# Attention stage of a gated-mix kernel: which queue issues which transfer, gate rows of all blocks in one step, the last tile turned in one row

## Chip, cores, metric

The kernel runs on one core of one Trainium2 chip. The metric is the device time of one execution in microseconds (us). Engines are named as in the profile: PE is TensorE's matrix multiplication, PEld its weight load, DVE VectorE, ACT ScalarE, POOL GpSimd, SP SyncE, whose only work here is to issue DMAs.

## What is computed

`x` is 2048 tokens x 576. Branch A is a linear attention with 32 heads of 18 features, branch B a gated feed-forward layer of 4608 hidden features; a sigmoid of one logit per token mixes the two. Everything is float32.

```python
qkv = x @ wqkv                                  # per head: q, k, v
pq, pk = q @ w_phi, k @ w_phi                   # 18 x 18 per head
phi_q = concat([softmax(pq), softmax(-pq)])     # 36 features per head
phi_k = concat([softmax(pk), softmax(-pk)])
kv  = einsum("bhsf,bhsd->bhfd", phi_k, v);  z = phi_k.sum(over tokens)
num = einsum("bhqf,bhfd->bhqd", phi_q, kv)
den = einsum("bhqf,bhf->bhq", phi_q, z) + 1e-6
a = (num / den) @ wo
gate = x @ W_gate; h = gate * (gate > 0) * (x @ W_up); b = h @ W_down
g = sigmoid((x * gate_w).sum(-1))
out = g * a + (1 - g) * b
```

## The kernel before

**Stages.** The first part, to about 404 us, is the attention; the rest is the feed-forward layer, in which TensorE works almost without a pause (1222 of the last 1232 us). Tokens come in 16 tiles of 128 and in 4 blocks of 512; the blocks' attention is finished in the order 3, 0, 1, 2, so "block 0" below is the first in that order.

**Keys, values, query features.** Per tile TensorE projects keys, values and queries, VectorE and ScalarE make the softmax features, and `kv_step` sums the products of key features and values. The query features `e` of a tile (128 tokens x 1152) are needed with features on the partitions: `turn` transposes them in eleven pieces of 128 x 108 in three groups (4, 4 and 3) into PSUM, and ScalarE copies each group out. For the last four tiles that copy goes straight into the operand `ph` of the sums. For the first twelve it goes to a tile `et`, which a DMA stores to DRAM (`eT`, 594 KB each); `fetch` reads four of them back as one block's `ph` (four DMAs of 594 KB).

**Sums and division.** `sums` multiplies `ph` with the summed key-value products `kvm`: six results per block, in the order 4, 5, 3, 2, 1, 0. ScalarE copies each to SBUF (`R`, for the fifth `og`). The numerators stand in the rows of `R`, the denominators in a few rows between them; small DMAs of 4 to 12 KB collect the denominators into `dn` (SP's queue), and others, of 28 to 40 KB, bring rows that lie in `og` into the free rows of `R` (`R<-og`, GpSimd's queue). `gate_rows` spreads the block's gates over 128 x 128 (`gx`, VectorE) and TensorE transposes them. `invert` takes the reciprocal of `dn` on VectorE, multiplies it by the gate rows, changes its layout from 128 x 128 to 32 x 512 with one DMA of 64 KB (`kt<-dn`, SP's queue), and splits the result into a high and a low half, `rd` (ScalarE, then VectorE). `divide` spreads `rd` over the rows of `R` by a matmul with `spread`; VectorE multiplies, ScalarE and VectorE split the quotients into `oh` and `ol`. `first_out` and `project_out` multiply them with `wo`; `rows_out` copies the result to a tile `o` and stores it to DRAM as `att`, which the feed-forward part reads back much later. The tiles `o` (and `sb`, a row spread that is stored as `sbd`) come from the pool `tb_`, which has four buffers.

**Loads for the feed-forward part in the same stage.** `load_operand` reads sums of `x` back (`xr<-xt`, 768 KB each), `load_in_place` and `load_rests` read `xo<-xt` (512 KB) and `xr<-xt` (256 KB), `load_w` weights (`wr<-wgu`, 768 KB). All are issued by SP.

**What sets the order.** From the last tiles on the program is written out by hand inside `in_order`: TensorE, SP and GpSimd carry out their instructions exactly as written, and a DMA that has to wait for its data holds up all that stands behind it in its engine's queue. VectorE and ScalarE are ordered by a scheduler, apart from the places marked `after`. The piece of the written order around block 0's inversion reads:

```python
        turn(FIRST - 2, 2, turned(kv_bank(0)))
        g0 = gate_rows(0, kv_bank(1))
        fetch(BLOCKS[2], nc.gpsimd)
        final = query_steps(FIRST - 1, eng=nc.vector)
        next(final)
        invert(0, g0)
        ...
        sums(1, (4,), (kv_bank(0),))
        sums(1, (5,), (kv_bank(1),))
```

and the one that follows the last tile: `load_operand(0, 0)`, `load_operand(0, 1)`, `fetch(BLOCKS[3])`, `first_out(2)`, `sums(2, (4, 5))`, `divide(0, 0)`, `invert(1)`. Names in the profile are those of the tiles; a line is the one that issues the instruction (L382 the store of `et`, L421 the fetch, L542 and L544 `dn`, L546 and L549 `R<-og`, L571 `kt<-dn`, L573 `rd`, L737 `att`, L751 to L786 the loads of `x` sums, L804 `wr`).

Of the kernel before, what the change touches and what calls it, by code (L numbers as in the profile page):

```python
# [14 lines left out]
DH = D // H  # L15
# [68 lines left out]
def gated_mix_kernel(  # L84
# [102 lines left out]
    def softmax_parts(ps, out):  # L187

        p = ps[:, :, :D // 2].rearrange("p c (h f) -> p c h f", f=DH)
        mx = soft.tile([P, H], F32, name="mx")  # L190
        mn = soft.tile([P, H], F32, name="mn")
        by2 = lambda a: a.rearrange("p (c h) -> p c h", c=2)
        wide = lambda a: by2(a)[:, :, :, None].to_broadcast([P, 2, H // 2, DH])
        nc.vector.tensor_reduce(out=by2(mx), in_=p, axis=AX, op=ALU.max)
        nc.vector.tensor_reduce(out=by2(mn), in_=p, axis=AX, op=ALU.min)
        yield
        e = ep.tile([P, H, 2, DH], F32, name="e")
        e2 = e.rearrange("p (c h) s f -> p c h s f", c=2)
        tt(out=e2[:, :, :, 0], in0=p, in1=wide(mx), op=SUB)
        tt(out=e2[:, :, :, 1], in0=wide(mn), in1=p, op=SUB)  # L200
        nc.scalar.activation(e, e, AF.Exp)
        yield
        sm = soft.tile([P, H, 2], F32, name="sm")
        nc.vector.tensor_reduce(out=sm.rearrange("p h s -> p (h s)"), in_=e.rearrange("p h s f -> p (h s) f"),  # L204
                                axis=AX, op=ADD)
        out.extend((e, sm))
# [157 lines left out]
    def turn(t, b, ps=None):  # L364

        gg = QN[b]
        if ps is None:
            ps = pv1.tile([QK, 4, P], F32, name="ptr", tag="pv1")
        for i, g in enumerate(gg):
            nc.tensor.transpose(ps[:, i], flat(EQ[t])[:, QC[g]:QC[g] + QK], ident)  # L370
        if t >= FIRST:
            nc.scalar.activation(PH[t // 4][:, t % 4, gg.start:gg.stop], ps[:, :len(gg)], AF.Copy)
        else:
            if t not in ET:
                ET[t] = etp.tile([QK, NQ, P], F32, name="et")
            a = ET[t][:, gg.start:gg.stop], ps[:, :len(gg)]
            nc.scalar.activation(*a, AF.Copy)
        TURNED[t] = TURNED.get(t, 0) + 1
        if TURNED[t] == 3:
            EQ.pop(t)  # L380
            if t < FIRST:
                nc.sync.dma_start(eT[t * QK:(t + 1) * QK], ET.pop(t).rearrange("p g t -> p (g t)"))  # L382

# [67 lines left out]
    for t in range(2, NT - 2):  # L451
# [10 lines left out]
        if t == 12:  # L462
# [5 lines left out]
            kt_p = RS.enter_context(tc.tile_pool(name="kt_p", bufs=1, **R_))  # L468
            kt_ = kt_p.tile([P, NJ * QK + 120], F32, name="kt")
            kt = kt_[:, :NJ * QK].rearrange("p (g c) -> p g c", g=NJ)  # L470
# [56 lines left out]
    def sums(b, ii, pp_):  # L527
# [9 lines left out]
        for i, ps in zip(ii, pp_):  # L537
            n = P if i < NJ - 1 else QM
            og = (OG4[b] if i == 4 else R[:, i if i < 4 else 4])[:n]
            nc.scalar.activation(og, ps[:n], AF.Copy)  # L540
            if i < NJ - 1:
                nc.sync.dma_start(dn[4 * HG * i:4 * HG * (i + 1)], og[64 - QH:64 + QH])  # L542
            else:
                nc.sync.dma_start(dn[4 * HG * i:], og[:2])  # L544
            if i < 4:
                nc.gpsimd.dma_start(R[QG:QG + 2 * GAP, i], OG4[b][i // 2 * 74 + i % 2 * 20:][:20])  # L546
            elif i == 5:
                for r, c in ((0, 40), (14, 114)):
                    nc.gpsimd.dma_start(R[r:r + 14, 4], OG4[b][c:c + 14])  # L549
            if i == 0:  # L550
                PH.pop(BLOCKS[b])

    RD, OW = {}, {}

    def gate_rows(b, ps):

        c = 4 * BLOCKS[b]
        gx = rb.tile([P, H, 4], F32, name="gx", bufs=1)
        nc.vector.tensor_copy(gx, gs[:, None, c:c + 4].to_broadcast([P, H, 4]))
        nc.tensor.transpose(ps[:, :P], gx.rearrange("p h c -> p (h c)"), ident)  # L560
        return ps[:, :P]

    def invert(b, g=None):

        dn = DN.pop(b)
        if g is None:
            g = gate_rows(b, kv_bank(0))
        nc.vector.reciprocal(dn, dn)
        tt(out=dn, in0=g, in1=dn, op=MULT)
        d2 = kt_[:H, :TB]  # L570
        nc.sync.dma_start(d2, dn)  # L571
        rd = RD[b] = rb.tile([2 * H, TB], F32R, name="rd", bufs=1)
        nc.scalar.activation(rd[:H], d2, AF.Copy)  # L573
# [59 lines left out]
    with in_order(tc, nc, nc.tensor, nc.sync, nc.gpsimd):  # L633
# [48 lines left out]
        turn(FIRST - 2, 2, turned(kv_bank(0)))  # L682
        g0 = gate_rows(0, kv_bank(1))
        fetch(BLOCKS[2], nc.gpsimd)
        final = query_steps(FIRST - 1, eng=nc.vector)
        next(final)
        invert(0, g0)
        halves = last_of(nc, nc.scalar), last_of(nc, nc.vector)
        two = pp.tile([P, 2, TB], F32, name="po", tag="pp")
        sums(1, (4,), (kv_bank(0),))  # L690
        sums(1, (5,), (kv_bank(1),))
        sums(1, (3, 2), (two[:, 0], two[:, 1]))
        next(final)
# [3 lines left out]
        sums(1, (1,), (kv_bank(2),))  # L697
        sums(1, (0,), (pv1.tile([P, TB], F32, name="po", tag="pv1"),))
        divide(0, 3)
        two = pp.tile([P, 2, TB], F32, name="pw", tag="pp")  # L700
# [6 lines left out]
        two = pp.tile([P, 2, TB], F32, name="po", tag="pp")  # L707
        turn(FIRST - 1, 2, turned(kv_bank(0)))
        for b in range(2):
            turn(FIRST - 1, b, turned(two[:, b]))  # L710
        divide(0, 1)
# [9 lines left out]
    def root_rows(tb):  # L721

        sb = tb_.tile([P, TB], F32, name="sb", tag="tb")
        on_all_rows(kv_bank(0), sb, tb)
        nc.sync.dma_start(sbd[:, tb], sb)

    def rows_out(b, m, ps):
# [9 lines left out]
        (nc.sync if b == NTB - 1 else nc.gpsimd).dma_start(att[m * P:m * P + n, BLOCKS[b] * TB:(BLOCKS[b] + 1) * TB], o)  # L737

# [8 lines left out]

    def load_operand(hf, i):
        if i < len(SEQ):
            XR[hf, i] = xr.tile([P, 3, TB], F32, name="xr", tag="xr")  # L750
            nc.sync.dma_start(XR[hf, i], xt[:, hf, SEQ[i] - 1])  # L751

# [125 lines left out]
    def operand_ahead(i):  # L878
# [4 lines left out]
        if i == 0:  # L883
            load_operand(0, 2)

# [6 lines left out]
    with in_order(tc, nc, nc.tensor, nc.sync, nc.gpsimd):  # L892
        x0, x1, x2 = (operand_ahead(i) for i in range(3))
        load_operand(0, 0)
        load_operand(0, 1)
        fetch(BLOCKS[3])
        first_out(2, range(5))
        halves = two[:, 0], two[:, 1]
        sums(2, (4, 5), halves)
        divide(0, 0)  # L900
        invert(1)
        first_out(1, range(5))
        sums(2, (3, 2), halves)
        divide(1, 4)
        for m in range(5):
# [4 lines left out]
            if m == 3:  # L910
                divide(1, 2)
        sums(2, (1, 0), halves)
        divide(1, 1)
        divide(1, 0)
        for m in range(5):
            project_out(1, m)
            if m < 3:
                two = pp.tile([P, 2, TB], F32, name="po", tag="pp")
                sums(3, ORDER[2 * m:2 * m + 2], (two[:, 0], two[:, 1]))
            if m == 0:  # L920
                invert(2)
            else:
                divide(2, 5 - m)
# [4 lines left out]
            if m == 4:  # L928
                divide(2, 0)
                invert(3)  # L930
                whole(x1)
        for m in range(5):
# [630 lines left out]
```

## Time and profile before

| | |
|---|---|
| time, median of 3 runs | 1643.85 us (1640.85 to 1646.56) |
| the profiled execution | time 1644.79 us, span 1643.0 us, mean granted clock 0.984 |
| busy, of the span | PE 1594.9 us (97%), PEld 1325.0 (81%), DVE 1198.9 (73%), ACT 561.8 (34%), POOL 177.4 (11%) |
| DMA | 284.43 MB, mean 173 GB/s |
| chain that ended last | PE 87%, DVE 6%, DMA 3%, ACT 2% |

The profile is of one execution. An engine's busy time counts its compute instructions; DMA issues, waits and branches don't count. "Granted clock" is the share of full speed that TensorE had. The chain is followed back from the last instruction, at each step to what released it. A row with x4 stands for four instructions in a row of the same line, operation and shape.

### The profile page before, as it was taken

To read this page: it belongs to the slowest core of one execution; us is meant where nothing else is said; L and a number is where in the kernel's file an instruction comes from. 1 tells how busy PE (TensorE), PEld (TensorE's weight loads), DVE (VectorE), ACT (ScalarE), POOL (GpSimd) and SP (SyncE) were. 2 spreads that over 40 slices of the span, in tenths; PEclk is the share of its full clock that TensorE was granted. 3 is DMA by queue.
4 is the path that set the end of the run, shared out by engine and by line. 5 is a ranking of instruction groups with operands and counts; after the bars stand their busy time and mean duration, and the time that the engine had idled before them with its cause. 6 is when DMAs were issued, how large, how long until landed. Compare 5 with 4: busy or idle time off the path is not lost.

```text
span 1643.0 us, 20184 instructions
## 1 busy us (share of the span) xinstructions
PE 1594.9 (97%) x7823; PEld 1325.0 (81%) x7823; DVE 1198.9 (73%) x1856; ACT 561.8 (34%) x921; POOL 177.4 (11%) x261
## 2 busy tenths in 40 slices
PE   9998998788999999999999999999999999999998
PEld 8898995456888888888888887778888888888887
DVE  4898775346778787788777777667777677777777
ACT  4343334344333333333233234223232323223231
POOL 0128212110000000000000002111111111111110
PEclk9899998899999999999999999999999999999999
DMA  8154305428775566555654543554343434344342
GB/s 266 65 180 157 113 24 150 149 87 313 260 257 198 208 234 241 203 211 208 222 204 177 201 158 116 176 216 155 140 168 139 185 127 182 127 171 153 146 163 72
DMA packets 64587, 284.43 MB, mean 173 GB/s; under 512 B 7018, under 2 KB 17514, under 8 KB 55788
## 3 DMA queue, kind: packets, MB, share of 16 engines
q1 hardware_dynamic: 61532, 275.25, 45.9%
q0 software_dynamic: 2384, 6.86, 1.4%
q8 instruction: 61, 1.00, 0.2%
q10 hardware_dynamic: 576, 1.05, 0.2%
q14 instruction: 34, 0.28, 0.0%
HBM read 172.51 MB, written 109.21 MB: 171 GB/s over the span
## 4 chain that ended last, share of the span: by engine, by line
PE 87%; DVE 6%; DMA 3%; ACT 2%; issue 2%; POOL 0%; SPq 0%; DVEq 0%; ACTq 0%; POOLq 0%
PE cx L1060 27%; PE ca L1060 13%; PE pd L1100 12%; PE pd L1123 10%; PE cy L1060 7%; PE kv L175 3%; PE pq L175 2%; PE pm L1100 2%; PE pm L1123 2%; PE pk L175 2%; PE pw L175 1%; DMA kt<-dn 1%; PE pv L237 1%; DVE sm L204 1%; DMA wdr<-wd 1%
## 5 line engine op out<-in xcount | busy, mean ns | idle before, releaser
L1167 ACT ACTIVATE hh<-g 128x512 fp32r<-128x512 f32 x195 | 119.9, 624 | 459.2 <-DVE g L1217 289.9
L1138 DVE TENSOR_TENSOR ac<-pd,ac 128x512 f32<-128x512 f32 x238 | 164.0, 689 | 145.4 <-PE pd L1123 145.2
L1060 PE MATMUL cx<-xo,wb 128*128 128x512 f32 x1008 | 252.1, 393 | 4.3 <-DVE u L1342 3.5
L1060 PE MATMUL cx<-xo,ws 128*128 128x512 f32 x1008 | 252.5, 390 | 2.9 <-ACT g L1221 2.8
L1060 PE MATMUL ca<-xo,ws 128*128 128x512 f32 x1008 | 252.0, 389 | 0.6 <-DMA ws<-wsd 0.6
L1060 PEld LDWEIGHTS cx<-xo,wb 128*128 128x128 f32 x1008 | 190.1, 190 | 46.5 <-DVE u L1342 4.4
L1060 PEld LDWEIGHTS cx<-xo,ws 128*128 128x128 f32 x1008 | 189.0, 188 | 43.6 <-ACT g L1221 4.6
L1060 PEld LDWEIGHTS ca<-xo,ws 128*128 128x128 f32 x1008 | 189.4, 188 | 40.2 <-issue 1.0
L1100 PE MATMUL pd<-hh,wd 128*128 128x512 f32 x576 | 200.8, 389 | 0.0
L1123 PE MATMUL pd<-hh,wd 128*128 128x512 f32 x476 | 185.4, 390 | 0.0
L1106 DVE TENSOR_TENSOR ac<-pd,ac 128x512 f32<-128x512 f32 x144 | 99.0, 688 | 105.5 <-PE pd L1100 103.2
L1172 DVE TENSOR_TENSOR hl<-g,hh 128x512 fp32r<-128x512 f32 x195 | 136.2, 699 | 1.9 <-ACT hh L1167 0.2
L1221 ACT ACTIVATE g<-cx 128x512 f32<-128x512 f32 x144 | 84.6, 588 | 128.0 <-PE cx L1060 127.9
L1100 PEld LDWEIGHTS pd<-hh,wd 128*128 128x128 f32 x576 | 108.2, 188 | 22.5 <-DVE ac L1106 0.2
L1060 PE MATMUL cy<-xo,wb 128*128 128x512 f32 x504 | 125.9, 389 | 0.0
L1023 ACT ACTIVATE wd<-wdr 128x384 fp32r<-128x384 f32 (+1 forms) x106 | 62.3, 607 | 152.1 <-DMA wdr<-wd 152.1
L1100 PE MATMUL pd<-hl,wd 128*128 128x512 f32 x288 | 112.2, 390 | 1.0 <-ACT xo L792 1.0
L1060 PEld LDWEIGHTS cy<-xo,wb 128*128 128x128 f32 x504 | 94.7, 188 | 19.6
L1123 PEld LDWEIGHTS pd<-hh,wd 128*128 128x128 f32 x476 | 89.4, 188 | 18.6
L1123 PE MATMUL pd<-hl,wd 128*128 128x512 f32 x238 | 92.6, 389 | 0.0
L776 POOL TENSOR_TENSOR xo<-xr,xo 32x512 fp32r<-32x512 f32 x5 | 8.2, 1655 | 639.3 <-DVE xo L776 631.7
L1026 DVE TENSOR_TENSOR wd<-wdr,wd 128x384 fp32r<-128x384 f32 (+1 forms) x106 | 69.5, 670 | 5.4 <-ACT wd L1023 5.4
(247 smaller groups left out, 2606.1 us busy)
## 6 DMA issues: line engine op xcount, KB each, us to landing
wsd<-ws SPq DMA_DIRECT2D x34, 1280.0 KB
ws<-wsd SPq DMA_DIRECT2D x34, 1280.0 KB
wbd<-wb SPq DMA_DIRECT2D x34, 960.0 KB
wb<-wbd SPq DMA_DIRECT2D x34, 960.0 KB
wr<-wgu SPq DMA_DIRECT2D x36, 768.0 KB
wdr<-wd SPq DMA_DIRECT2D x36, 576.0 KB
eT<-et SPq DMA_DIRECT2D x12, 594.0 KB
xt<-xb SPq DMA_DIRECT2D x7, 768.0 KB
```

The lines of the kernel that those rows point to most:

```text
L175: nc.tensor.matmul(ps, w, m, start=i == 0, stop=i == len(pairs) - 1)
L204: nc.vector.tensor_reduce(out=sm.rearrange("p h s -> p (h s)"), in_=e.rearrange("p h s f -> p (h s) f"), axis=AX, op=ADD)
L1023: nc.scalar.activation(o[:, 0], a, AF.Copy)
L1026: tt(out=o[:, 1], in0=a, in1=o[:, 0].bitcast(F32), op=SUB)
L1060: nc.tensor.matmul(ps, w, v, start=first and m == 0, stop=m == len(pairs) - 1, skip_group_check=True)
L1100: nc.tensor.matmul(ps, w, v, start=k == 0 and (i < 2 or first), stop=k == len(mms) - 1 and (i < 2 or last), skip_group_check=True)
L1106: tt(out=a, in0=ps, in1=a, op=ADD)
L1123: mm = lambda ps, w, v, a, z: nc.tensor.matmul(ps, w, v, start=a, stop=z, skip_group_check=True)
L1138: tt(out=a, in0=ps, in1=a, op=ADD)
L1167: nc.scalar.activation(h, src, AF.Copy)
L1172: tt(out=l, in0=src, in1=h.bitcast(F32), op=SUB)
L1221: nc.scalar.activation(a, ps, AF.Copy)
```

## The change

Four things, all in the attention stage:

1. The gathers `R<-og` move from GpSimd's queue to SP's, in batches written out by a new function `gather`; the stores of `att` of all blocks are now SP's (before, only the last block's). The stores of `et` of tiles 10 and 11, the last fetch, the first three `xr<-xt` and the stores `sbd` move from SP's queue to GpSimd's.
2. The gate rows of all four blocks are made once, before block 0's inversion: GpSimd copies the gates into 128 x 512 (`gx`), TensorE makes four transposes, ScalarE copies the result into `gT`, the upper half of the tile whose lower half takes `kt<-dn`.
3. `invert` is cut in two, `invert` (to the DMA) and `split_inverse` (from `rd` on); for block 0, the two first sums of block 1 are written between them. For the other blocks the second follows the first directly.
4. For tile 11 the eleven transposes stand in a row and the three copies after them; before, each group's transposes were followed by its copy.

```diff
 
-        gg = QN[b]
-        if ps is None:
-            ps = pv1.tile([QK, 4, P], F32, name="ptr", tag="pv1")
-        for i, g in enumerate(gg):
-            nc.tensor.transpose(ps[:, i], flat(EQ[t])[:, QC[g]:QC[g] + QK], ident)
-        if t >= FIRST:
-            nc.scalar.activation(PH[t // 4][:, t % 4, gg.start:gg.stop], ps[:, :len(gg)], AF.Copy)
-        else:
-            if t not in ET:
-                ET[t] = etp.tile([QK, NQ, P], F32, name="et")
-            a = ET[t][:, gg.start:gg.stop], ps[:, :len(gg)]
-            nc.scalar.activation(*a, AF.Copy)
+        turn_all(t, [(b, pv1.tile([QK, 4, P], F32, name="ptr", tag="pv1") if ps is None else ps)])
+
+    def turn_all(t, bb):
+
+        for b, ps in bb:
+            for i, g in enumerate(QN[b]):
+                nc.tensor.transpose(ps[:, i], flat(EQ[t])[:, QC[g]:QC[g] + QK], ident)
+        for b, ps in bb:
+            gg = QN[b]
+            if t >= FIRST:
+                o = PH[t // 4][:, t % 4]
+            else:
+                if t not in ET:
+                    ET[t] = etp.tile([QK, NQ, P], F32, name="et")
+                o = ET[t]
+            nc.scalar.activation(o[:, gg.start:gg.stop], ps[:, :len(gg)], AF.Copy)
+        TURNED[t] = TURNED.get(t, 0) + len(bb) - 1
         TURNED[t] = TURNED.get(t, 0) + 1
         if TURNED[t] == 3:
             EQ.pop(t)
             if t < FIRST:
-                nc.sync.dma_start(eT[t * QK:(t + 1) * QK], ET.pop(t).rearrange("p g t -> p (g t)"))
+                (nc.sync if t < FIRST - 2 else nc.gpsimd).dma_start(eT[t * QK:(t + 1) * QK], ET.pop(t).rearrange("p g t -> p (g t)"))
 
...
             kt_p = RS.enter_context(tc.tile_pool(name="kt_p", bufs=1, **R_))
-            kt_ = kt_p.tile([P, NJ * QK + 120], F32, name="kt")
+            kt_ = kt_p.tile([P, 2 * TB], F32, name="kt")
+            gT = kt_[:, TB:]
             kt = kt_[:, :NJ * QK].rearrange("p (g c) -> p g c", g=NJ)
...
                 nc.sync.dma_start(dn[4 * HG * i:], og[:2])
-            if i < 4:
-                nc.gpsimd.dma_start(R[QG:QG + 2 * GAP, i], OG4[b][i // 2 * 74 + i % 2 * 20:][:20])
-            elif i == 5:
-                for r, c in ((0, 40), (14, 114)):
-                    nc.gpsimd.dma_start(R[r:r + 14, 4], OG4[b][c:c + 14])
             if i == 0:
                 PH.pop(BLOCKS[b])
 
     RD, OW = {}, {}
 
-    def gate_rows(b, ps):
-
-        c = 4 * BLOCKS[b]
-        gx = rb.tile([P, H, 4], F32, name="gx", bufs=1)
-        nc.vector.tensor_copy(gx, gs[:, None, c:c + 4].to_broadcast([P, H, 4]))
-        nc.tensor.transpose(ps[:, :P], gx.rearrange("p h c -> p (h c)"), ident)
-        return ps[:, :P]
-
-    def invert(b, g=None):
+    def gather(b, *kk):
+
+        R = RW[b]
+        for k in kk:
+            if k < 4:
+                nc.sync.dma_start(R[QG:QG + 2 * GAP, k], OG4[b][k // 2 * 74 + k % 2 * 20:][:20])
+            else:
+                for r, c in ((0, 40), (14, 114)):
+                    nc.sync.dma_start(R[r:r + 14, 4], OG4[b][c:c + 14])
+
+    def gate_rows():
+
+        gx = ep.tile([P, H, 2, DH], F32, name="gx", tag="e").rearrange("p h s f -> p (h s f)")[:, :TB]
+        nc.gpsimd.tensor_copy(gx.rearrange("p (b h c) -> p b h c", b=NTB, h=H),
+                              gs.rearrange("p (b c) -> p b c", b=NTB)[:, :, None].to_broadcast([P, NTB, H, 4]))
+        ps = kv_bank(1)
+        for b in range(NTB):
+            nc.tensor.transpose(ps[:, b * P:(b + 1) * P], gx[:, b * P:(b + 1) * P], ident)
+        nc.scalar.activation(gT, ps, AF.Copy)
+
+    def invert(b):
 
         dn = DN.pop(b)
-        if g is None:
-            g = gate_rows(b, kv_bank(0))
         nc.vector.reciprocal(dn, dn)
-        tt(out=dn, in0=g, in1=dn, op=MULT)
+        tt(out=dn, in0=gT[:, BLOCKS[b] * P:(BLOCKS[b] + 1) * P], in1=dn, op=MULT)
         d2 = kt_[:H, :TB]
         nc.sync.dma_start(d2, dn)
+
+    def split_inverse(b):
+
+        d2 = kt_[:H, :TB]
         rd = RD[b] = rb.tile([2 * H, TB], F32R, name="rd", bufs=1)
...
         turn(FIRST - 2, 2, turned(kv_bank(0)))
-        g0 = gate_rows(0, kv_bank(1))
+        gate_rows()
         fetch(BLOCKS[2], nc.gpsimd)
         final = query_steps(FIRST - 1, eng=nc.vector)
         next(final)
-        invert(0, g0)
-        halves = last_of(nc, nc.scalar), last_of(nc, nc.vector)
+        gather(0, 4, 3, 2)
+        invert(0)
+        gather(0, 1, 0)
         two = pp.tile([P, 2, TB], F32, name="po", tag="pp")
         sums(1, (4,), (kv_bank(0),))
         sums(1, (5,), (kv_bank(1),))
+        with after(tc, nc, nc.scalar, last_of(nc, nc.scalar)):
+            split_inverse(0)
+        halves = last_of(nc, nc.scalar), last_of(nc, nc.vector)
         sums(1, (3, 2), (two[:, 0], two[:, 1]))
...
         sums(1, (0,), (pv1.tile([P, TB], F32, name="po", tag="pv1"),))
+        gather(1, 4, 3, 2, 1, 0)
         divide(0, 3)
...
         two = pp.tile([P, 2, TB], F32, name="po", tag="pp")
-        turn(FIRST - 1, 2, turned(kv_bank(0)))
-        for b in range(2):
-            turn(FIRST - 1, b, turned(two[:, b]))
+        turn_all(FIRST - 1, [(2, turned(kv_bank(0))), (0, turned(two[:, 0])), (1, turned(two[:, 1]))])
         divide(0, 1)
...
         on_all_rows(kv_bank(0), sb, tb)
-        nc.sync.dma_start(sbd[:, tb], sb)
+        nc.gpsimd.dma_start(sbd[:, tb], sb)
 
...
             tt(out=o, in0=c, in1=ps[:64], op=ADD)
-        (nc.sync if b == NTB - 1 else nc.gpsimd).dma_start(att[m * P:m * P + n, BLOCKS[b] * TB:(BLOCKS[b] + 1) * TB], o)
+        nc.sync.dma_start(att[m * P:m * P + n, BLOCKS[b] * TB:(BLOCKS[b] + 1) * TB], o)
 
...
 
-    def load_operand(hf, i):
+    def load_operand(hf, i, queue=nc.sync):
         if i < len(SEQ):
             XR[hf, i] = xr.tile([P, 3, TB], F32, name="xr", tag="xr")
-            nc.sync.dma_start(XR[hf, i], xt[:, hf, SEQ[i] - 1])
+            queue.dma_start(XR[hf, i], xt[:, hf, SEQ[i] - 1])
 
...
         if i == 0:
-            load_operand(0, 2)
+            load_operand(0, 2, nc.gpsimd)
 
...
         x0, x1, x2 = (operand_ahead(i) for i in range(3))
-        load_operand(0, 0)
-        load_operand(0, 1)
-        fetch(BLOCKS[3])
+        load_operand(0, 0, nc.gpsimd)
+        load_operand(0, 1, nc.gpsimd)
+        fetch(BLOCKS[3], nc.gpsimd)
         first_out(2, range(5))
         halves = two[:, 0], two[:, 1]
         sums(2, (4, 5), halves)
         divide(0, 0)
         invert(1)
+        split_inverse(1)
         first_out(1, range(5))
...
         sums(2, (1, 0), halves)
+        gather(2, 4, 3, 2, 1, 0)
         divide(1, 1)
...
                 sums(3, ORDER[2 * m:2 * m + 2], (two[:, 0], two[:, 1]))
+            if m == 2:
+                gather(3, 4, 3, 2, 1, 0)
             if m == 0:
                 invert(2)
+                split_inverse(2)
             else:
...
                 invert(3)
+                split_inverse(3)
                 whole(x1)
```

Three places show how the queues change. The first is SP's queue around the inversions of blocks 0 and 1 (`kt<-dn`), before:

```order
L542 DMA dn<-R 24x1x128 x4
L382 DMA eT<-et 108x1408
L571 DMA kt<-dn 32x4x128
L542 DMA dn<-og 24x1x128
L544 DMA dn<-R 8x1x128
L542 DMA dn<-R 24x1x128 x4
L382 DMA eT<-et 108x1408
L751 DMA xr<-xt 128x1536 x2
L421 DMA ph<-eT 108x1408 x4
L542 DMA dn<-og 24x1x128
L544 DMA dn<-R 8x1x128
L571 DMA kt<-dn 32x4x128
```

The same stretch of SP's queue after:

```order
L548 DMA dn<-R 24x1x128 x4
L564 DMA R<-og 14x512 x2
L561 DMA R<-og 20x512 x2
L582 DMA kt<-dn 32x4x128
L561 DMA R<-og 20x512 x2
L548 DMA dn<-og 24x1x128
L550 DMA dn<-R 8x1x128
L548 DMA dn<-R 24x1x128 x4
L564 DMA R<-og 14x512 x2
L561 DMA R<-og 20x512 x4
L548 DMA dn<-og 24x1x128
L550 DMA dn<-R 8x1x128
```

The two stores `eT`, the two `xr` and the four `ph` are gone from it; in their stead stand the gathers `R<-og`, and block 1's `kt<-dn` is the next row after the last shown. The second place is GpSimd's queue in the same stretch (its last product for a tile's features, L209, to the first stores), before:

```order
L209 TENSOR_TENSOR e<-e,r 128x32x18
L549 DMA R<-og 14x512 x2
L546 DMA R<-og 20x512 x4
L421 DMA ph<-eT 108x1408 x4
L549 DMA R<-og 14x512 x2
L546 DMA R<-og 20x512 x4
L549 DMA R<-og 14x512 x2
L546 DMA R<-og 20x512 x2
L737 DMA att<-o 128x512 x4
```

and after:

```order
L209 TENSOR_TENSOR e<-e,r 128x32x18
L387 DMA eT<-et 108x1408
L569 COPY gx<-gates 128x512
L426 DMA ph<-eT 108x1408 x4
L387 DMA eT<-et 108x1408
L769 DMA xr<-xt 128x1536 x2
L426 DMA ph<-eT 108x1408 x4
L743 DMA sbd<-sb 128x512 x2
L769 DMA xr<-xt 128x1536
```

GpSimd's queue now holds transfers of 256 to 768 KB alone, and the copy of the gates stands in it between the store of tile 10 and the first fetch. The third place is SP's queue later, from the inversion of block 3 (the first row) to the loads for the feed-forward part, before:

```order
L571 DMA kt<-dn 32x4x128
L804 DMA wr<-wgu 128x1536
L781 DMA xo<-xt 128x1024
L786 DMA xr<-xt 128x512 x3
L804 DMA wr<-wgu 128x1536
L781 DMA xo<-xt 128x1024 x3
L786 DMA xr<-xt 128x512
L737 DMA att<-o 128x512 x4
```

and after:

```order
L582 DMA kt<-dn 32x4x128
L755 DMA att<-o 128x512 x2
L822 DMA wr<-wgu 128x1536
L799 DMA xo<-xt 128x1024
L804 DMA xr<-xt 128x512 x3
L822 DMA wr<-wgu 128x1536
L799 DMA xo<-xt 128x1024 x3
L804 DMA xr<-xt 128x512
L755 DMA att<-o 128x512 x2
L755 DMA att<-o 64x512
```

The stores of `att` of block 2, which GpSimd issued, now stand in SP's queue: two ahead of the loads, three behind them.

More of the change, by code (lines that the diff above doesn't have):

```diff
@@ L196, in softmax_parts @@
         yield
-        e = ep.tile([P, H, 2, DH], F32, name="e")
+        e = ep.tile([P, H, 2, DH], F32, name="e", tag="e")
         e2 = e.rearrange("p (c h) s f -> p c h s f", c=2)
```

## The prediction

> **What bounds the kernel now.** I read the page first. Its chain by line lists TensorE's work almost alone, the feed-forward lines (L1060, L1100, L1123) above all; one small transfer, `kt<-dn`, is the only DMA of the attention stage on it:
>
> ```profile
> PE cx L1060 27%; PE ca L1060 13%; PE pd L1100 12%; PE pd L1123 10%; PE cy L1060 7%; PE kv L175 3%; PE pq L175 2%; PE pm L1100 2%; PE pm L1123 2%; PE pk L175 2%; PE pw L175 1%; DMA kt<-dn 1%; PE pv L237 1%; DVE sm L204 1%; DMA wdr<-wd 1%
> ```
>
> Then the stages (columns: length; busy us of PE, PEld, DVE, ACT, POOL with counts; granted clock; DMA share; GB/s). These four are where the change acts:
>
> ```profile
> 263.70:277.00 13.30, 7.67 (x44) 4.97 (x44) 4.35 (x8) 2.57 (x5) 3.74 (x7) 0.86 0.88 228
> 277.00:287.00 10.00, 9.99 (x21) 4.52 (x22) 6.10 (x12) 5.46 (x9) 3.07 (x6) 0.50 0.23 59
> 304.70:312.50 7.80, 0.05 (x3) 0.01 (x1) 0.68 (x1) 1.71 (x3) 1.48 (x3) 0.68 0.52 194
> 312.50:321.00 8.50, 7.81 (x15) 4.22 (x15) 2.06 (x3) 3.24 (x6) 2.10 (x5) 0.50 0.22 77
> ```
>
> TensorE stands idle for 5.6 us of the first row (13.30 − 7.67) and for all 7.8 of the third, and after each the granted clock is 0.50 for a while. The chain in order of time (start, us, what) names what it waits for; both times the 64 KB of inverted sums take almost 9 us from the issue until ScalarE can go on:
>
> ```profile
> 266.62 8.82 DMA kt<-dn
> ...
> 277.01 0.66 PE kv L585
> ...
> 300.76 0.60 ACT R L540
> ...
> 302.16 8.91 DMA kt<-dn
> ...
> 312.49 0.68 PE kv L585
> ```
>
> Why 9 us? The timeline of SP and GpSimd gives what was issued around them, and the third such transfer, with no bulk near it:
>
> ```profile
> 264.35 0.31 SPq L382 DMA_DIRECT2D eT<-et  x1
> 266.30 2.21 POOL L421 DMA_DIRECT2D ph<-eT  x4
> ...
> 293.54 1.36 SPq L751 DMA_DIRECT2D xr<-xt  x2
> 295.00 3.29 SPq L421 DMA_DIRECT2D ph<-eT  x4
> ...
> 333.15 0.62 SPq L571 DMA_DIRECT2D kt<-dn  x1
> ...
> 335.38 0.63 ACT L573 ACTIVATE rd<-kt 32x512 fp32r<-32x512 f32 x1 [2.65 <-DMA kt<-dn]
> ...
> kt<-dn SPq DMA_DIRECT2D x4, 64.0 KB
> ...
> ph<-eT POOLq DMA_DIRECT2D x4, 594.0 KB, 9.4
> ```
>
> Left alone it takes 335.38 − 333.15 = 2.23 us. The two slow ones differ: the second has its bulk ahead of it **on its own queue** (`ph<-eT`, 4 × 594 KB = 2.4 MB, and two `xr<-xt`), the first mostly **on the other queue** (GpSimd's `ph<-eT`, as large), with one `eT<-et` ahead on its own. The queues' shares of the DMA engines from 270 to 277, and, for the second, the rate from 302 to 309 (packets, MB, share) show it, with the mean rate ahead:
>
> ```profile
> DMA packets 502, 1.64 MB, mean 234 GB/s; under 512 B 75, under 2 KB 225, under 8 KB 502
> q0 software_dynamic: 333, 1.56, 94.1%
> q1 hardware_dynamic: 169, 0.08, 6.0%
> ...
> DMA packets 425, 2.00 MB, mean 286 GB/s; under 512 B 40, under 2 KB 72, under 8 KB 425
> ```
>
> While the first `kt<-dn` crawls, SP's queue moves 0.08 MB and GpSimd's takes 94% of the engines. That is the arrangement which the change makes for the second one too.
>
> **The change part by part.** *Block 0's layout change (place 1).* The gate rows are now made by GpSimd, behind the store of tile 10, and TensorE turns them ahead of the last query projection. Rows for it:
>
> ```profile
> 262.61 1.72 ACT L377 ACTIVATE et<-kv 108x512 f32<-108x512 f32 x3 [0.36 <-PE kv L370]
> ...
> L476 POOL CAST spread<-ones 64x640 fp32r<-64x640 f32 x1 | 0.7, 707 | 0.0
> ...
> L209 POOL TENSOR_TENSOR e<-e,r 128x576 f32<-128x576 f32 x14 | 17.3, 1237 | 55.2 <-DVE r L356 34.5 <-ACT vt L291 13.6 <-ACT ph L372 7.1
> ```
>
> The copies that fill `et` end at 264.33; GpSimd issues the store (2.21 / 4 = 0.55), then copies 128x512: 0.57 by the cast (707 ns for 640 columns) to 1.10 by the two-operand form (1237 for 576); I take 0.7, the nearer kind, so 265.6. Four transposes 0.65 (row below at 291.80), ScalarE's copy 0.60 and VectorE's product 0.3 put the issue of `kt<-dn` at about 267.4 instead of 266.62: **+0.8**. TensorE waits for it: the last query projection and block 1's first sums, queued behind the four transposes, start about 2.5 us later than now, which the 5.6 us of idle time covers (without that cover they would cost the 2.5). On GpSimd the four `ph<-eT` queue behind the copy, 0.7 later and not needed before block 2's sums. Also ahead of `kt<-dn` on SP now stand four gathers, which wait for `dn<-R` to land; the reciprocal waits for the same. Its duration: bounds 2.23 (alone) and 8.82 (against GpSimd's bulk); bulk is still there and starts earlier, so I keep 8.82.
>
> *Block 1's (place 2).* Gone is the bulk on its own queue; it now runs on GpSimd's. Same bounds, 2.23 to 8.82, nearest row the first `kt<-dn`. That one had a 594 KB store ahead on its own queue, this one only small things, so I take 7.5: 8.91 − 7.5 = **−1.4** (from 0 to −6.7). The Trainium skill, "DMA: Bandwidth & Descriptors", section "Issuing engines are not separate DMA queues", says that transfers from sync, scalar and gpsimd run on the same 16 engines and interleave, so several issuers save only issue time: by it this term is 0, and the trace's 94.1% agrees.
>
> *TensorE's own work:*
>
> ```profile
> 291.80 0.65 PE L370 MATMUL po<-ident,e 128*108 128x128 f32 x4 [0.69 <-ACT et L377]
> ...
> 330.73 0.33 PE L560 MATMUL kv<-ident,gx 128*128 128x128 f32 x1
> 331.44 0.65 PE L320 MATMUL kv<-ident,gates 128*128 128x128 f32 x4 [0.38 <-DVE dn L569]
> ...
> 352.50 0.62 SPq L571 DMA_DIRECT2D kt<-dn  x1
> 355.36 0.60 ACT L732 ACTIVATE o<-pw 128x512 f32<-128x512 f32 x1 [2.41 <-PE pw L175]
> 355.85 0.61 ACT L573 ACTIVATE rd<-kt 32x512 fp32r<-32x512 f32 x1
> ```
>
> Eleven transposes in a row lose the wait of 0.69: **−0.7**, on the path, since the divisions behind them lead to 300.76. Block 2's gate rows vanish with their wait: 0.33 + 0.38, **−0.7**. Of block 3's nothing counts on TensorE, which waits for `rd` afterwards; but `rd<-kt` stands on ScalarE behind `o<-pw`, which TensorE now reaches sooner, and the data would be there at 352.50 + 2.23 = 354.7 against 355.85: up to −1.1, less what two `att` stores now ahead on SP's queue cost: **−0.5** (−1.1 to +1). VectorE loses four copies of `gx`, at most 0.5 each, beside waits: nothing.
>
> *The stores of `att` and the loads.* On SP's queue they stand between small transfers and loads (place 3):
>
> ```profile
> 364.07 0.56 POOL L737 DMA_DIRECT2D att<-o  x1 [7.26 <-ACT o L732]
> 368.49 0.34 SPq L804 DMA_DIRECT2D wr<-wgu  x1
> ...
> 375.47 0.32 SPq L786 DMA_DIRECT2D xr<-xt  x1
> ...
> 381.40 0.60 ACT L732 ACTIVATE o<-kv 128x512 f32<-128x512 f32 x1 [1.52 <-PE kv L175]
> 383.84 1.49 ACT L809 ACTIVATE ws<-wr 128x1536 fp32r<-128x1536 f32 x1 [1.85 <-DVE wr L833]
> ...
> 382.00:384.00 2.00, 2.00 (x10) 1.65 (x10) 1.70 (x4) 0.16 (x1) 0.00 (x0) 1.00 1.00 399
> 384.00:386.00 2.00, 2.00 (x11) 1.65 (x10) 0.64 (x1) 2.00 (x2) 0.00 (x0) 1.00 0.70 269
> ...
> att<-o POOLq DMA_DIRECT2D x1, 256.0 KB, 2.6
> ...
> att<-o POOLq DMA_DIRECT2D x1, 256.0 KB, 7.1
> ```
>
> The two stores ahead of `wr<-wgu` are ready by 364, so the loads aren't held. But three stores of block 2 now queue behind the loads, whose last is issued at 375.47. All transfers end near 385.4 (0.70 of the last slice), five stores among them, 1.15 MB or 2.9 us at 399 GB/s: the loads alone end near 382.5, and a store behind them lands 1 to 2 us later, about 384. Its buffer is one of four, and ScalarE's second `o` of block 3 (381.40) waits for it; behind that stands `ws<-wr`, which has slack until 383.84. So 384 + 0.6 − 383.84 = about **+0.6** (0 to +3.5), passed on by VectorE, which is busy from there to the feed-forward part.
>
> The sum: +0.8 − 1.4 − 0.7 − 0.7 − 0.5 + 0.6 = −1.9, made against the profiled execution (span 1643.0, time 1644.79); beside the median of 1643.85 it gives **1642 us**.
>
> **The rivals.** *A, faster: the small transfers really are free of the bulk.* For it: the second one's bulk is all on its own queue; against it: 94.1% to 6.0% above. At 2.23 us block 0 restarts when TensorE's own sums end, 2.5 us later than now, near 274 (−3.0); block 1 gains 8.91 − 2.23 = 6.7; and of the busy 9.99 and 7.81 us at clock 0.50 a quarter could go (half is the most, and the divisions also wait for VectorE): −4.5. With the other terms (−1.3) −15.5, 1628 us. At about 5 us each, block 0 still restarts at 274 (267.4 + 5 + 1.5), −3.0, block 1 gains 3.9, and only the first stretch its quarter, 2.5: −10.7, **1633**. The Trainium skill, "TensorE: Matmul & The Clock Gate", Part 1, has the clock halve after an idle window of about 3.4 us and return after a busy one; the idle gaps of 5.6 and 7.8 us followed by 0.50 agree.
>
> *B, slower: the stores behind the loads.* For it: a store beside loads took 7.1 us, alone 2.6. It decides from a landing at 387 on: ScalarE's `ws<-wr` then starts at 387.6 instead of 383.84 (+3.8), TensorE waits 3.3 us for the bank, and if the clock drops as in the row of 312.50, whose 7.81 busy us would be 3.9 at full rate, another 3.5. With −2.5 from the other terms +4.8: **1648.7**. Against it: the loads end before 385.
>
> *C, slower: the gathers.* They share SP's queue with `kt<-dn` under GpSimd's bulk; that bulk moves at 234 GB/s where SP's moved at 286, so it lasts longer. If `kt<-dn` lands 3 us later in block 0 and 2 later in block 1, and half clock lasts 3.4 us more (+1.7): +3 + 2 + 1.7 − 1.3 = +5.4, **1649**.
>
> *D: the queues change nothing for `kt<-dn`*, as the skill's rule has it: the sum without −1.4, −0.5, 1643.3.
>
> **How the numbers follow.** Forecast 0.30, D 0.16, A 0.32, B 0.12, C 0.10. A measurement of this kernel can tell about 0.3%, 4.9 us, from no change. The forecast spills 0.02 to the fast side: faster 0.34, same 0.44, slower 0.22. The range reaches down to A's full case, 1628, whose price of the half clock is the least known, and up to C, 1649; sums of B with C are left out. The likeliest cases alone: 1639 to 1646.
>
> **What would show it.** In the chain of the changed kernel: `kt<-dn` of block 0 issued near 267.4 and of 8 to 9 us, of block 1 near 7.5; both clock stretches at 0.50 still there; no wait ahead of the last four transposes; ScalarE's `o` of block 3 waiting for a DMA near 384. I am wrong if either `kt<-dn` takes under 5 us, if the clock stays at 1.00 after 277, or if the feed-forward part starts more than 5 us away from 403.8.

## The result and the profile after

The changed kernel takes 1647.68 us (median of 16 runs, 1646.38 to 1650.73), the kernel before 1642.68 (16 runs, 1637.36 to 1648.38): a ratio of 1.0032, 95% interval 1.0021 to 1.0043, 5.0 us (3.4 to 7.1) **slower**. The forecast was 1.9 us faster; the time lies in the range and the sign is wrong. The profiled execution takes 1647.01 us (span 1644.9).

The chain of waits of the changed kernel (start, us, what), with the rows that answer to those of before:

```profile
266.36 10.95 DMA kt<-dn
...
278.82 0.66 PE kv L600
...
302.89 11.05 DMA kt<-dn
...
315.36 0.69 PE kv L600
...
335.40 2.41 DMA kt<-dn
...
377.00 9.25 DMA att<-o
...
386.34 0.61 ACT o L750
...
406.72 5.09 PE cx L1084 x14
```

The feed-forward part begins, in the kernel before, with this row of the chain:

```profile
403.83 6.25 PE cx L1060 x14
```

Both slow layout changes got longer, 8.82 to 10.95 and 8.91 to 11.05, where the forecast kept the first and shortened the second; the third, with no bulk beside it, takes 2.41 as before. A new wait for a store of `att` stands ahead of ScalarE's `o`. The feed-forward part starts 2.9 us later. The stages (columns as in the prediction) show the same; the second and fourth row follow the two waits:

```profile
263.70:277.00 13.30, 9.51 (x46) 6.83 (x46) 3.57 (x6) 1.79 (x3) 2.67 (x5) 0.87 0.94 236
277.00:287.00 10.00, 8.18 (x18) 3.81 (x19) 6.22 (x12) 6.48 (x10) 0.00 (x0) 0.56 0.13 31
304.70:312.50 7.80, 0.00 (x0) 0.00 (x0) 0.00 (x0) 1.00 (x2) 0.00 (x0) 0.77 0.99 223
312.50:321.00 8.50, 4.95 (x9) 2.51 (x10) 2.33 (x4) 2.34 (x4) 0.00 (x0) 0.50 0.20 66
```

In the third, TensorE is idle for all 7.8 us with the DMA engines 99% busy, and the half clock follows it as before. What those engines move there stands in the DMA shares by queue from 302.9 to 313.9 us, the whole second `kt<-dn` (SP's queue is q1, GpSimd's q0):

```profile
DMA packets 692, 2.35 MB, mean 213 GB/s; under 512 B 105, under 2 KB 295, under 8 KB 691
## 3 DMA queue, kind: packets, MB, share of 16 engines
q0 software_dynamic: 471, 2.23, 87.8%
q1 hardware_dynamic: 220, 0.10, 4.8%
```

SP's queue, free of bulk now, moved 0.10 MB in 11 us. How it did so shows in two of these microseconds, 310 to 312:

```profile
DMA packets 178, 0.48 MB, mean 239 GB/s; under 512 B 15, under 2 KB 101, under 8 KB 178
q0 software_dynamic: 89, 0.43, 90.1%
q1 hardware_dynamic: 89, 0.04, 11.1%
```

The two queues moved 89 packets each, but GpSimd's ten times the bytes. In the kernel before, with the bulk ahead on the same queue, SP's queue moved 57 packets of 0.32 MB from 308 to 309 us and 210 of 0.18 MB in the next: there the small packets came when the bulk was over.

### The profile page after: what moved, and what is told of

Same layout as the page of the kernel before. It is cut to its first block, busy times and chain, and to the rows that moved or that the text cites. A ratio compares the mean times of both kernels' runs of the same rounds, so it can differ in the third digit from the quotient of the medians.

```text
span 1644.9 us, 20158 instructions
## 1 busy us (share of the span) xinstructions
PE 1592.0 (97%) x7823; PEld 1322.1 (80%) x7823; DVE 1198.4 (73%) x1852; ACT 562.9 (34%) x922; POOL 163.9 (10%) x234
## 4 chain that ended last, share of the span: by engine, by line
PE 84%; DVE 5%; DMA 5%; ACT 2%; issue 2%; SPq 1%; POOL 1%; POOLq 0%; ACTq 0%; DVEq 0%
PE cx L1084 27%; PE ca L1084 13%; PE pd L1124 12%; PE pd L1147 10%; PE cy L1084 7%; PE kv L175 2%; PE pq L175 2%; PE pm L1124 2%; PE pm L1147 2%; PE pk L175 2%; DMA kt<-dn 2%; DMA wdr<-wd 1%; DVE sm L204 1%; PE pv L237 1%; PE ptr L372 1%
## 5 line engine op out<-in xcount | busy, mean ns | idle before, releaser
L1084 PEld LDWEIGHTS cy<-xo,wb 128*128 128x128 f32 x504 | 94.6, 188 | 19.6
```

The source lines that it names most:

```text
L1084: nc.tensor.matmul(ps, w, v, start=first and m == 0, stop=m == len(pairs) - 1, skip_group_check=True)
```

## The experiments

The numbers behind the verdicts are gathered here: `kt` is the time from the issue to the start of ScalarE's `rd<-kt`, or the row of the chain, for blocks 0, 1 and 2 ("<": ScalarE did not wait for it); "bulk" is the first issue of the bulk at block 1's transfer (the store of tile 11's `eT`, followed by the loads), "landing" the start of `rd<-kt` after that issue; FF is the start of the feed-forward part (the row `cx` ahead of which TensorE waits for `u`). Ratios are against the runs of the kernel before that were taken beside each (medians from 1642.55 to 1643.88).

| kernel | kt block 0 | block 1 | block 2 | bulk | landing | FF | median us | ratio (95%) |
|---|---|---|---|---|---|---|---|---|
| before | 8.82 | 8.91 | 2.23 | SP, 293.11 | 18.0 | 403.83 | 1642.68 | |
| before_again | 8.57 | 9.98 | 2.17 | SP, 292.61 | 19.1 | 404.00 | 1643.44, one run | |
| changed | 10.95 | 11.05 | 2.41 | GpSimd, 294.61 | 19.4 | 406.72 | 1647.68 | 1.0032 (1.0021–1.0043) |
| after_again | 10.65 | 10.75 | 2.39 | GpSimd, 292.98 | 19.0 | 405.56 | 1646.68, one run | |
| old_queues | 8.54 | 10.46 | 2.17 | SP, 290.92 | 19.0 | 401.76 | 1644.14 | 1.0009 (0.9996–1.0021) |
| gathers0_behind | 10.90 | 11.28 | 2.40 | GpSimd, 293.64 | 19.6 | 405.42 | 1647.28 | 1.0028 (1.0017–1.0039) |
| fetch_behind | <6.4 | 10.88 | 2.40 | GpSimd, 285.80 | 19.2 | 399.23 | 1639.79 | 0.9981 (0.9967–0.9995) |
| xr_late | 10.70 | 6.97 | 6.13 | GpSimd, 294.55 | 15.3 | 405.99 | 1648.44 | 1.0027 (1.0012–1.0041) |
| xr_same_queue | 10.57 | 7.10 | 2.45 | GpSimd, 293.52 | 15.4 | 404.35 | 1642.79 | 1.0001 (0.9990–1.0011) |
| att_gpsimd | 10.30 | 11.68 | 2.50 | GpSimd, 294.12 | 20.0 | 412.06 | 1652.35 | 1.0052 (1.0034–1.0070) |
| att2_gpsimd | 10.60 | 10.57 | 2.38 | GpSimd, 297.03 | 18.9 | 407.79 | 1646.07 | 1.0017 (1.0004–1.0031) |
| bulk_behind | 3.59 | 2.27 | 2.22 | behind | | 395.10 | 1634.88 | 0.9951 (0.9936–0.9966) |
| small_first | <3.9 | <2.6 | 2.20 | behind | | 387.63 | 1627.52 | 0.9903 (0.9881–0.9925) |
| six_buffers | <3.9 | <2.6 | 2.20 | behind | | 386.02 | 1624.92 | 0.9884 (0.9867–0.9901) |

**Is it the queues at all? old_queues.** The changed kernel, but

```diff
-  nc.sync.dma_start(R[...], OG4[b]...)           # gathers, SP
+  nc.gpsimd.dma_start(R[...], OG4[b]...)       # where the kernel before has them, block 0's behind gx
-  (nc.sync if t < FIRST - 2 else nc.gpsimd).dma_start(eT...)
+  nc.sync.dma_start(eT...)
-  load_operand(0, 0, nc.gpsimd); load_operand(0, 1, nc.gpsimd); fetch(BLOCKS[3], nc.gpsimd)
+  load_operand(0, 0); load_operand(0, 1); fetch(BLOCKS[3])     # load_operand(0, 2) and sbd on SP, att of blocks 0-2 on GpSimd too
```

> The changed kernel with every transfer issued by the engine that issued it in the kernel before; gate rows made once, the eleven transposes and the split inversion stay. Theory Q (the queues cost the time): the two kt<-dn take about 8.8 and 8.9 us as before, the second o of block 3 waits for no store, the feed-forward part starts at 402 to 404 us, and the time is 0 to 2 us below the kernel before. Theory E (the other edits, gate rows and order, cost it): the time stays 4 to 6 us above the kernel before, and the first kt<-dn is still followed by its divide at about 278.8.

Theory Q holds for the time: 8.54 us again for block 0, the feed-forward part at 401.76, no store waited for, and 1.0009 (0.9996 to 1.0021) instead of 1.0032. It missed block 1's transfer: that took 10.46 with its bulk ahead of it on SP's queue, not the 8.9 expected, and so nearly the changed kernel's 11.05. What the queues cost in these traces is the 2.4 us of block 0's transfer and the wait for the store. Its profile starts the feed-forward part 2.1 us sooner than before, as the other edits should; its times don't show that gain, and don't exclude one of 0.7 us.

**The gathers, or the bulk? gathers0_behind.**

```diff
-        gather(0, 4, 3, 2)
         invert(0)
-        gather(0, 1, 0)
+        gather(0, 4, 3, 2, 1, 0)
```

> The changed kernel with block 0's six gathers behind its kt<-dn in SP's queue instead of four ahead of it. Theory B (bulk on the other queue shares the engines until it has ended): kt<-dn still ends with the bulk at about 277.3, so it takes 10 to 11 us, and the time stays within 1 us of the changed kernel. Theory G (the gathers ahead of it on its own queue stretch it): it takes 8 to 9 us or less, its divide comes 2 to 3 us sooner, and the time falls by as much.

10.90 us with none of the gathers ahead of it: theory G falls for block 0. **fetch_behind** takes the bulk away from block 0's transfer instead:

```diff
         gate_rows()
-        fetch(BLOCKS[2], nc.gpsimd)
...
         invert(0)
         gather(0, 1, 0)
+        fetch(BLOCKS[2])
```

> The changed kernel with fetch(BLOCKS[2]) moved from GpSimd's queue, where it runs beside block 0's kt<-dn, to SP's queue behind that transfer and its gathers. Theory B: block 0's kt<-dn, beside the store of tile 10 alone, takes 2.5 to 5 us instead of 10.95, the first divide starts at 273 to 275 instead of 278.8, block 1's kt<-dn stays at 10 to 11 us, and the time falls by 3 to 6 us against the changed kernel. Rival (block 1's small transfers, now behind the fetch on SP's queue, hold TensorE instead): the time falls by less than 2 us.

ScalarE no longer waits for block 0's `kt<-dn` (`rd<-kt` starts at 272.35 behind other work of its own), and the kernel is 8 us faster than the changed one (1639.79; 3 to 6 were expected). Block 1's transfer is issued 8.8 us sooner and still takes 10.88, with its bulk there too: it lands 19.2 us after that bulk begins, like the other rows with the same bulk (18.0 to 20.0).

**Amount and queue: xr_late and xr_same_queue.** Two `xr<-xt` of 768 KB leave block 1's bulk for a place beside block 2's transfer: in xr_late on GpSimd's queue, in xr_same_queue on SP's, behind it. TensorE's, ScalarE's and VectorE's instructions stand in the same order in both.

```diff
-        load_operand(0, 0, nc.gpsimd)
-        load_operand(0, 1, nc.gpsimd)
         fetch(BLOCKS[3], nc.gpsimd)
...
                 root_rows(m + 2)                 # xr_late
+            if m == 0:
+                load_operand(0, 0, nc.gpsimd)
+                load_operand(0, 1, nc.gpsimd)
...
                 split_inverse(2)                 # xr_same_queue instead
+                load_operand(0, 0)
+                load_operand(0, 1)
```

> The changed kernel with the first two xr<-xt (768 KB each) moved on GpSimd's queue from before the last fetch to behind the first sbd store, which waits for its data until about 335. Block 1's kt<-dn then meets 3.0 MB of bulk (one eT store, four ph<-eT) instead of 4.5 MB. Theory B (the transfer lands when the bulk on the other queue has moved): it lands about 1.5 MB at 237 GB/s = 6.6 us sooner, near 307, and takes 4 to 5 us instead of 11.05; the time falls by 5 to 8 us against the changed kernel. Rival (a fixed price for bulk on the other queue, whatever its amount): it still takes 10 to 11 us and the time stays.

> xr_late with one thing changed: the same two xr<-xt stand on SP's queue directly behind block 2's kt<-dn instead of on GpSimd's queue, which issued them 0.2 us after it. Theory F (own queue keeps order, another queue takes turns): block 2's kt<-dn takes 2.2 to 3 us instead of 6.13, block 1's stays near 7, and the time falls by 3 to 5 us against xr_late. Rival (it is the load on the engines that counts, whichever queue it is on): block 2's kt<-dn stays at 5 to 6.5 us and the time stays.

With a third less bulk block 1's transfer lands 15.3 instead of 19.4 us after its start: 6.97, between the two expectations of 4 to 5 and 10 to 11, and the amount counts. The time did not fall by the 5 to 8 us expected (1.0027 against 1.0032): what was gained there was lost at block 2, whose `kt<-dn` had been undisturbed. The row of the chain of xr_late:

```profile
331.27 6.13 DMA kt<-dn
```

and of the timeline of its GpSimd (start, us of issuing):

```profile
331.49 1.08 POOL L769 DMA_DIRECT2D xr<-xt  x2
```

The bulk was issued after the small transfer and still made it 2.5 times as long. The same two loads directly behind it on its own queue, in the timeline of SP of xr_same_queue:

```profile
330.32 0.62 SPq L582 DMA_DIRECT2D kt<-dn  x1
331.02 1.10 SPq L769 DMA_DIRECT2D xr<-xt  x2
```

and the transfer in its chain:

```profile
330.32 2.45 DMA kt<-dn
```

Theory F holds: 6.13 against 2.45 us for the same 64 KB beside the same 1.5 MB, and 1648.44 against 1642.79 us (ratios 1.0027 and 1.0001). The turns can be counted, too: in xr_late from 334.5 to 335.5 us

```profile
q0 software_dynamic: 63, 0.39, 93.4%
q1 hardware_dynamic: 64, 0.03, 10.8%
```

One thing beside the queue differs: the loads came 0.22 us after the transfer in xr_late and 0.70 in xr_same_queue. No run changes that delay alone, so how much of the 3.7 us a later start on GpSimd's queue would have saved is open. The Trainium skill, "DMA: Bandwidth & Descriptors", section "Queues, rings and completion order", says that each DMA engine takes turns between the queues that have work, a whole packet each, and consumes one queue's descriptors in order; the packet counts agree with the first half, 6.13 against 2.45 with both.

**The stores of att: att_gpsimd and att2_gpsimd.**

```diff
-        nc.sync.dma_start(att[...], o)
+        (nc.sync if b == NTB - 1 else nc.gpsimd).dma_start(att[...], o)   # att_gpsimd
+        (nc.gpsimd if b == 2 else nc.sync).dma_start(att[...], o)         # att2_gpsimd
```

> The changed kernel with the att stores of blocks 0 to 2 issued by GpSimd again. If the stores behind the loads cost what the trace shows, ScalarE's second o of block 3 starts at about 383.4 instead of 386.3, the feed-forward part at about 405.8 instead of 406.7, and the time falls by about 1 us. If stores were the main cost of the change in most executions, it falls by 3 us or more; if VectorE sets that start anyway, by nothing.

> The changed kernel with the att stores of block 2 alone issued by GpSimd; the order on TensorE, ScalarE and VectorE up to the feed-forward part stays. If the stores behind the loads cost what the trace shows, ScalarE's second o of block 3 starts at about 383.4 instead of 386.3, the feed-forward part about 0.9 us sooner, and the time falls by about 1 us. If they were the main cost in most executions, it falls by 3 us or more.

att_gpsimd tells nothing about its question: the edit made the scheduler put ScalarE's `b<-pw` of block 0 behind two copies of sums (`R`) and three splits (`oh`), and TensorE waited for its bank. ScalarE's timeline has the copy at

```profile
329.24 0.59 ACT L753 ACTIVATE b<-pw 64x512 f32<-64x512 f32 x1
```

where the changed kernel has it at 324.30, and TensorE's (the wait ahead in brackets) the matmuls behind it at

```profile
330.69 1.62 PE L175 MATMUL pw<-oh,wo 128*128 128x512 f32 x3 [2.87 <-DVE o L754]
```

att2_gpsimd keeps that order. Its second `o` of block 3 waits for TensorE alone, and from block 3's `rd<-kt` (359.79) to the feed-forward part are 48.00 us; in the changed kernel 48.86 (from 357.86), in the kernel before 47.98 (from 355.85). So the stores behind the loads cost 0.9 us in the traces (49.05 against 47.99 in after_again and before_again); the medians do not show it, since the intervals of 1.0017 and 1.0032 overlap.

**The bulk behind the small: bulk_behind, small_first, six_buffers.** bulk_behind is the kernel before with two moves:

```diff
-        fetch(BLOCKS[2], nc.gpsimd)
...
         invert(0, g0)
+        fetch(BLOCKS[2])
...
-        load_operand(0, 0)
-        load_operand(0, 1)
-        fetch(BLOCKS[3])
...
         invert(1)
+        load_operand(0, 0)
+        load_operand(0, 1)
+        fetch(BLOCKS[3])
```

> The kernel before with the bulk behind both layout changes on SP's queue: fetch(BLOCKS[2]) behind the kt<-dn of block 0, and the two xr<-xt with fetch(BLOCKS[3]) behind that of block 1. Theory B (any bulk on the engines, ahead or on the other queue, is what makes kt<-dn 9 to 11 us): both take 2.2 to 4 us, TensorE goes on near 274 and 306 instead of 277.0 and 312.5, less of the time is at clock 0.50, and the time falls by 9 to 15 us against the kernel before, to 1628 to 1634. Rival (the bulk only moves: what follows waits for it): the small transfers of the next block stand behind the bulk, TensorE waits for them instead, and the time falls by less than 4 us.

Both transfers are short, the clock stays at 1.00 in the stage that had 0.50, and the time falls by 7.7 us, less than the 9 to 15 expected. The stage after block 0's transfer:

```profile
277.00:287.00 10.00, 9.31 (x44) 6.90 (x43) 5.34 (x11) 2.90 (x5) 3.02 (x6) 1.00 0.34 105
```

The chain has the reason why it isn't more: what stands behind the bulk now waits for it.

```profile
266.29 3.59 DMA kt<-dn
...
297.66 11.71 DMA dn<-R
...
311.51 3.01 DMA att<-o
```

And TensorE's timeline what that costs:

```profile
315.44 1.62 PE L175 MATMUL pw<-oh,wo 128*128 128x512 f32 x3 [8.56 <-DVE o L736]
```

A gather on GpSimd waits until 309.39 for those denominators, the stores of `att` stand behind it, and TensorE loses 8.56 us. small_first (on old_queues) puts each bulk behind the small transfers that it met; six_buffers adds its last line:

```diff
-        fetch(BLOCKS[2], nc.gpsimd)
...
         invert(0)
+        fetch(BLOCKS[2])
...
-        load_operand(0, 0)
-        load_operand(0, 1)
-        fetch(BLOCKS[3])
...
         sums(2, (3, 2), halves)
+        fetch(BLOCKS[3])
...
         sums(2, (1, 0), halves)
+        load_operand(0, 0)
+        load_operand(0, 1)
...
-    tb_ = BS.enter_context(tc.tile_pool(name="tb", bufs=4, **L_))
+    tb_ = BS.enter_context(tc.tile_pool(name="tb", bufs=6, **L_))      # six_buffers alone
```

> The kernel of old_queues with each bulk behind the small transfers it met: fetch(BLOCKS[2]) on SP's queue behind block 0's kt<-dn, fetch(BLOCKS[3]) on SP's queue behind block 1's kt<-dn and block 2's first two collections of denominators, the two xr<-xt behind its last two. Theory B: both kt<-dn take 2.2 to 4 us, no dn<-R waits long behind bulk (11.7 us in bulk_behind), the att stores of block 0 aren't held, and the time is 13 to 18 us below the kernel before. Rival (another transfer becomes the late one, denominators of block 2 or ph of block 3): 5 to 9 us below, as in bulk_behind.

> small_first with six instead of four buffers for the tiles that the att stores read. If the stores of block 0, slowed by fetch(BLOCKS[3]) beside them, hold TensorE (2.96 us idle before 308.09, b<-pw waits 1.75 us for a store), the wait goes and the time falls by 2 to 4 us against small_first. If denominators or VectorE are late next, by less than 1.

small_first takes 1627.52 us, 1.0% under the kernel before. In its chain a store of `att` is the longest wait left, since `fetch(BLOCKS[3])` now runs beside it:

```profile
299.53 6.54 DMA att<-o
```

The last division of block 1 comes behind it. TensorE's timeline of small_first, and then that of six_buffers:

```profile
308.09 0.79 PE L605 MATMUL kv<-rd,spread 64*128 64x512 f32 x1 [2.96 <-DVE R L607]
```

```profile
308.00 0.49 PE L605 MATMUL kv<-rd,spread 64*128 64x512 f32 x1 [0.79 <-DVE R L607]
```

With six buffers the wait is 0.79 and the feed-forward part starts 1.6 us sooner. The 1624.92 us (0.9884, 0.9867 to 0.9901) are the fastest here; the step from small_first is smaller than the two intervals.

**How far one profile holds: before_again, after_again.** Nothing is edited.

> The kernel before, profiled once more. If its profile is representative, the two kt<-dn take 8 to 9.5 us again, the second o of block 3 waits for no store, and the feed-forward part starts at 403 to 405 us. If its median lies under its profiled execution because these transfers are often shorter, one of them takes under 8 us here.

> The changed kernel, profiled once more: both kt<-dn 10 to 11.5 us, the second o of block 3 waits for a store of att until 385 to 387, the feed-forward part starts at 405 to 408 us.

The transfers repeat within about 1 us. The feed-forward part starts 1.6 us later in this pair, 2.9 in the first, and the times of the four profiled executions differ by 3.2 and 2.2; the medians differ by 5.0. Some 2 us of it are in no profile taken here, and stay open.

## Why the prediction was wrong

- **Block 0's layout change, duration kept at 8.82: too short.** It took 10.95. The issue came 0.3 us earlier instead of 0.8 later (`gx` ended at 264.24, not 265.6), so the step cost +1.8 at `divide` (278.82 against 277.01) instead of +0.8. (The rows of the prediction add up to an issue at 267.15, not 267.4.) The bulk beside it decides, not the gathers ahead of it (gathers0_behind, fetch_behind). Why GpSimd's bulk, a store of `eT` more and started 2.1 us sooner, costs 2 us more than in the kernel before was not separated further.
- **Block 1's, −1.4: the step that failed.** The words "this one only small things, so I take 7.5" took what stands ahead in its own queue to be what counts. It took 11.05, and the step cost +2.1: 3.5 of the 4.8 us between the forecast of −1.9 and the +2.9 at the feed-forward part. With the same bulk ahead of it on SP's queue the transfer took 8.91, 9.98 and 10.46 (before, before_again, old_queues), beside it on GpSimd's 10.57 to 11.68 (six rows of the table): moving the bulk from ahead to beside gained nothing and lost about 1 us. The packets of 310 to 312 us show why the free queue did not help: they took turns with the bulk's. With a third less bulk it took 6.97. In all nine rows with the full bulk the transfer lands 18.0 to 20.0 us after the bulk begins, but it is also issued 8.2 to 9.1 us after it, so these rows do not tell whether its own issue matters.
- **TensorE's own work, −0.7, −0.7: the right way.** The wait of 0.69 ahead of the last transposes is gone from the chain. From `divide` of block 0 to the issue of block 1's `kt<-dn` are 24.07 us (278.82 to 302.89), before 25.15; from there on block 2's issue comes 20.04 after block 1's `divide`, before 20.66. Block 3's −0.5 came to −0.2 (355.85 − 333.15 against 357.86 − 335.40).
- **The stores of att, +0.6: right**, 0.9 (att2_gpsimd), by the wait that was named, though the store landed at 386.25, not near 384.
- The account at the feed-forward part: +1.8 − 1.1 + 2.1 − 0.6 − 0.2 + 0.9 = +2.9, the 406.72 − 403.83 of the traces. In the second pair, after_again against before_again, the same six steps are +3.2 − 3.6 + 0.8 + 0.0 + 0.1 + 1.1 = +1.6. So block 0 and the stores cost time and block 1 gains none in both, but a single step differs by up to 2.5 us between the pairs, and block 2's −0.6 shows in the first pair alone.
- **Rivals.** C had the sign, the two places and nearly the sizes (+3 and +2 against +1.8 and +2.1), and its 1649 is near the 1647.68; but that is luck, since the gathers that it named have no part in block 0's delay (gathers0_behind), and its slower bulk does not repeat: over the second `kt<-dn` the engines moved 242, 216 and 222 GB/s with the bulk on SP's queue (before, before_again, old_queues), 213 and 223 with it on GpSimd's (changed, after_again). D's mechanism, the queue changes nothing, is nearly what block 1 shows (10.46 against 11.05), not what block 0 does (8.54 against 10.95). Its sum without −1.4 and −0.5 is 1643.9; the 1643.3 leaves out the −1.4 alone. The sentence of the Trainium skill ("DMA: Bandwidth & Descriptors", section "Issuing engines are not separate DMA queues") that several issuers save only issue time agrees with block 1, and says nothing of the 6.13 against 2.45. A's condition never came about in the change. small_first made it true and arrived at 1627.52; that this is A's 1628 does not check A's sum, since small_first also leaves the gathers and the stores on GpSimd's queue.
- **The signs of being wrong** did not show: neither transfer took under 5 us, the clock was 0.56 after 277, and the feed-forward part came 2.9 us late. They were set for transfers that get shorter, not longer.

## What to carry to other kernels

In this kernel a small transfer on which engines wait was protected from bulk by standing ahead of it in the same queue (2.45 us), not by a queue of its own (6.13 us): on two queues their packets took turns, one for one. So look for the bulk that is under way when the small transfer is issued, and move its issue behind it, then look at once for the next small transfer, which now stands behind that bulk (`dn<-R`, 11.71 us in bulk_behind). In a trace, ask for the packets of each queue while the small transfer is under way: a queue that moves as many packets as the bulk's, but a tenth of its bytes, is not free of the bulk.

## What had not been expected of the hardware

A bulk load issued 0.2 us after a 64 KB transfer, on another queue, came with 6.13 us for it, against 2.45 with the same load 0.7 us behind it on its own queue. And the clock can take back part of what a wait gained: xr_same_queue brought block 3's `rd<-kt` 4.9 us forward against xr_late, but its wait before the divisions was 3.53 instead of 2.23 us, and the fourteen matmuls behind took 5.92 instead of 3.39 (the fourteen in xr_late's chain, and below them xr_same_queue's):

```profile
360.80 3.39 PE kv L175 x14
```

```profile
356.38 5.92 PE kv L175 x14
```

The granted clock over these two stretches (columns as in the prediction, the clock third from the end) was 1.00 and 0.54:

```profile
360.80:364.19 3.39, 3.39 (x15) 2.55 (x15) 3.31 (x5) 0.63 (x1) 0.00 (x0) 1.00 0.00 0
356.38:362.30 5.92, 5.92 (x15) 4.41 (x15) 3.48 (x5) 0.63 (x1) 0.00 (x0) 0.54 0.00 0
```

Of the 4.9 us, 1.9 were left at the next division (362.23 against 364.12). The waits are those ahead of the divisions in TensorE's timelines, again xr_late first:

```profile
360.12 0.68 PE L600 MATMUL kv<-rd,spread 64*64 64x512 f32 x2 [2.23 <-DVE rd L589]
```

```profile
355.26 1.11 PE L600 MATMUL kv<-rd,spread 64*64 64x512 f32 x2 [3.53 <-DVE rd L589]
```
